# The first level of a score tree taken from TensorE to GpSimd and VectorE, and the order around four points of TensorE's first rounds changed

## The chip, the cores and the metric

The kernel runs on one core of a Trainium2 chip. The metric is the device time of one execution in microseconds (us), the median of several. A "span" is the time from the first to the last instruction in one profiled execution, some 2 us less than the device time. All executions used below ran fast, unless one is called slow.

## The reference, cut to what matters

Attention of the RWKV6 kind over 4 batches, 8 heads, 768 steps and head size 48, then a normalisation and an MLP (384 to 1536 to 384), all in fp32.

```python
for t in range(S):
    cur = u * (k_t outer v_t)
    y[:, :, t] = r_t @ (state + cur)
    state = w_t[:, None] * state + k_t outer v_t
x = y as (B, S, H*D)
out = x + relu(layernorm(x) * g @ w_ch1) @ w_ch2
```

What matters: for an odd step t, the step just before it contributes (r_t . k_{t-1}) v_{t-1}. No decay w stands between two neighbours. All earlier steps come in with products of w.

## The kernel before: the parts concerned

There are eight rounds of 384 steps (a batch and a half of its steps). A round has two units of four heads. In a round the scores of steps inside blocks of 64 are built as a tree of six levels. Level 0 holds the neighbours, level 1 pairs of pairs, and so on. At each level TensorE multiplies (`quads`, into `a_ps`), VectorE multiplies r and k by the next products of w (`grow`, into `rkT`) and puts the scores into a matrix A (`keep`). The MLP of the round before (`h_ps`, `o_ps`) is cut into steps that fill TensorE between the levels.

```python
def own_products(q, eng):              # r*k*u of step t itself
    rk = st[q]["ruk"] = p1.tile([P, TT, NH, D], F32, tag="rk", ...)
    eng.tensor_tensor(out=rk, in0=k_of(q), in1=r_of(q), op=mult)     # names shortened
    eng.tensor_tensor(out=rk, in0=rk, in1=u_bc[...], op=mult)

def own_sums(q):
    o = st[q]["own"] = p4.tile([P, TT, NH], F32, tag="own", ...)
    DVE.tensor_reduce(out=o, in_=st[q]["ruk"], axis=AX.X, op=ALU.add)

def own_term(q, eng):                  # vo = v * own, added to y later
    eng.tensor_tensor(out=a["vo"], in0=vn[q], in1=own broadcast, op=mult)
...
for lev in range(NLEV):                # one round
    ...                                # states, outputs and MLP steps of the round before
    for q in now:
        if slot:
            quads(q, lev)
    ... grow(q, lev) ; keep(rnd, lev)
    ...
    if rnd == 2 and lev == 2:
        for q in now:
            take(DVE, q)               # own_products and own_sums, both on VectorE
    ...
    if lev == NLEV - 1 and rnd >= 2:   # what is prepared for the next round
        tasks += each(own_term, new[:1], [POOL])
        tasks += each(own_products, new[1:], [POOL])
        tasks += each(own_sums, new[1:]) + each(own_term, new[1:], [POOL])
        tasks += each(totals, [rnd + 1], [POOL])
```

The program fixes the order of instructions on each engine, so on VectorE a sum that waits for GpSimd's products holds up all that stands behind it. Two buffers named `nat["w"]`, which hold w as it lies in memory, have no use once round 1 has begun.

## Time and profile before

| | before |
|---|---|
| device time, median of the 3 runs known when predicting | 581.06 us (580.58 to 582.94) |
| span of the profiled execution | 579.2 us |
| busy: TensorE, VectorE, GpSimd | 560.5, 317.3, 94.5 us |
| mean granted clock of TensorE | 0.979 |

The busy time of TensorE is 97% of the span, so two things can shorten it: work taken from TensorE, and the stops and half-clock stretches of the first 217 us. The views that show both, line by line, are in the prediction. In the costliest groups, the columns after the bar are busy us and mean ns of one instruction:

```profile
L49 DVE TENSOR_TENSOR rkT<-rkT,wT 128x768 f32<-128x768 f32 x16 | 17.1, 1107 | 0.9 <-PE a_ps L49 0.8
```

This is `grow` of level 0. Two such products stand between a round's start and its level 1, and they read the tiles while GpSimd works beside them.

### The profile page before, as it was taken

The numbers are of one execution on the slowest core, as the hardware profiler recorded it, in microseconds if no ns is written. First come the engines' busy times: TensorE is split into PE (matmuls) and PEld (weight loads), VectorE is DVE, ScalarE is ACT, GpSimd is POOL, SyncE is SP. The second block draws the span as 40 slices with busy tenths as digits, with TensorE's granted clock in tenths as the row PEclk, the third lists the DMA queues.
The fourth block names the chain that finished last, engine by engine and source line by source line (L and its number), as shares of the span: only waits on it lengthen the run. The fifth ranks groups of instructions, "written<-read, shape, count | busy, mean of one in ns | idle before, by whom it ended". The sixth has DMA issues, their size and how long they took to land.

```text
span 579.2 us, 19006 instructions
## 1 busy us (share of the span) xinstructions
PE 560.5 (97%) x8378; PEld 370.7 (64%) x8378; DVE 317.3 (55%) x636; ACT 168.6 (29%) x363; POOL 94.5 (16%) x127
## 2 busy tenths in 40 slices
PE   9999989999979989999999999999999999999997
PEld 6776765666546656666666666666666666666554
DVE  4879888769767754558256654557253531130000
ACT  3576597402340015201241015301331025202200
POOL 6140010204062007100350007020420000000000
PEclk9889799999997989999999999999999999999999
DMA  9848587245564547345343534144000000000000
GB/s 231 194 114 166 124 234 179 53 93 101 147 135 89 132 98 138 68 115 120 95 86 82 134 85 89 36 116 103 15 3 2 15 29 2 1 15 29 0 14 27
DMA packets 109875, 50.78 MB, mean 88 GB/s; under 512 B 92768, under 2 KB 99040, under 8 KB 109792
## 3 DMA queue, kind: packets, MB, share of 16 engines
q1 hardware_dynamic: 107920, 48.98, 37.1%
q8 instruction: 65, 1.06, 0.8%
q10 hardware_dynamic: 1872, 0.59, 0.4%
q14 instruction: 18, 0.15, 0.1%
HBM read 42.76 MB, written 4.72 MB: 82 GB/s over the span
## 4 chain that ended last, share of the span: by engine, by line
PE 81%; DVE 6%; ACT 4%; SPq 3%; DMA 3%; issue 2%; POOL 0%; ACTq 0%; DVEq 0%
PE o_ps L49 30%; PE h_ps L49 27%; PE a_ps L49 10%; PE y L49 4%; DVE rkT L49 3%; PE kv L49 2%; SPq L163 2%; DMA v<-in_v_dram 2%; PE kn_ps L49 2%; PE xT_ps L49 1%; ACT rest L49 1%; PE own_ps L49 1%; SPq L173 1%; PE idle L49 1%; PE r_ps L49 1%
## 5 line engine op out<-in xcount | busy, mean ns | idle before, releaser
L49 PE MATMUL o_ps<-w_sb,h 128*128 128x384 f32 x576 | 201.0, 498 | 1.0 <-ACT h L49 1.0
L49 PE MATMUL h_ps<-xT,w_sb 128*128 128x384 f32 x576 | 197.3, 494 | 0.0
L49 PEld LDWEIGHTS o_ps<-w_sb,h 128*128 128x128 f32 x576 | 107.3, 193 | 67.9 <-issue 3.0
L49 PEld LDWEIGHTS h_ps<-xT,w_sb 128*128 128x128 f32 x576 | 106.7, 191 | 66.7 <-issue 1.2
L49 DVE TENSOR_TENSOR rkT<-rkT,tot 128x768 f32<-128x768 f32 (+1 forms) x96 | 79.3, 867 | 28.3 <-issue 15.5
L49 ACT ACTIVATE h<-h_ps 128x384 f32<-128x384 f32 x96 | 46.8, 488 | 151.3 <-PE h_ps L49 151.2
L49 PEld LDWEIGHTS a_ps<-rkT 48*64 48x64 f32 x4608 | 73.7, 137 | 24.3 <-issue 15.9
L49 PE MATMUL a_ps<-rkT 48*64 48x32 f32 x4608 | 79.1, 222 | 3.7 <-DVE s L49 3.0
L49 DVE TENSOR_TENSOR o<-o_ps,x 128x384 f32<-128x384 f32 x24 | 13.3, 555 | 103.2 <-PE o_ps L49 103.1
L49 POOL TENSOR_TENSOR vo<-v,own 128x576 f32<-128x576 f32 x16 | 19.2, 1203 | 258.5 <-DVE own L49 217.7
L49 DVE SCALAR_TENSOR_TENSOR s<-s,decay,kv 128x48 f32<-128x48 f32 x160 | 29.3, 258 | 33.9 <-PE kv L49 33.9
L49 ACT ACTIVATE rstd<-mv,eps 128x3 f32<-128x3 f32 x8 | 2.4, 296 | 134.8 <-DVE mv L49 134.8
L49 DVE COPY_PREDICATED A<-mask,a_ps 128x768 f32<-128x768 int8 x32 | 38.3, 1195 | 0.0
L49 DVE TENSOR_TENSOR x<-y,vo 128x288 f32<-128x288 f32 x32 | 13.2, 453 | 37.4 <-PE y L49 37.3
L49 ACT ACTIVATE xT<-xT_ps,g_sb 128x384 f32<-128x384 f32 x24 | 13.7, 580 | 55.3 <-PE xT_ps L49 55.3
L49 DVE TENSOR_REDUCE own<-rk 128x12 f32<-128x576 f32 x12 | 8.9, 746 | 20.6 <-POOL rk L49 20.6
L49 DVE TENSOR_SCALAR w_sb<-w_sb 128x384 f32<-128x384 f32 (+1 forms) x48 | 18.6, 388 | 0.8
L49 DVE STREAM_TRANSPOSE rkT<-r_runs 128x384 f32<-128x384 f32 x20 | 15.7, 837 | 4.3 <-DMA r_runs<-in_r_dram 4.3
L49 PEld LDWEIGHTS kv<-v,kn 64*64 64x64 f32 x768 | 12.7, 134 | 8.2 <-issue 6.2
L49 PEld LDWEIGHTS y<-v,A 64*64 64x64 f32 x384 | 13.3, 137 | 7.1 <-issue 4.4
L49 DVE TENSOR_TENSOR rkT<-rkT,wT 128x768 f32<-128x768 f32 x16 | 17.1, 1107 | 0.9 <-PE a_ps L49 0.8
L49 DVE STREAM_TRANSPOSE rkT<-k_runs 128x384 f32<-128x384 f32 x20 | 15.8, 849 | 1.7 <-DMA k_runs<-in_k_dram 1.6
(82 smaller groups left out, 501.4 us busy)
## 6 DMA issues: line engine op xcount, KB each, us to landing
raw<-in_moe_w_ch_dram SPq DMA_DIRECT2D x24, 384.0 KB, 3.7
w_runs<-in_w_dram SPq DMA_DIRECT2D x79, 70.0 KB, 2.1
k_runs<-in_k_dram SPq DMA_DIRECT2D x79, 70.0 KB, 2.0
r_runs<-in_r_dram SPq DMA_DIRECT2D x79, 70.0 KB, 2.0
v<-in_v_dram SPq DMA_DIRECT2D x48, 96.0 KB, 3.0
out_dram<-o SPq DMA_DIRECT2D x24, 192.0 KB, 2.8
nat_r<-in_r_dram SPq DMA_DIRECT2D x42, 96.0 KB, 3.3
nat_k<-in_k_dram SPq DMA_DIRECT2D x42, 96.0 KB, 3.2
```

The source lines that it names most:

```text
L49: return lambda *args, **kw: self.tc.keep_in_program_order(f(*args, **kw))
L163: eng.dma_start(out=t[ds(HP * j + SQ * e, SQ), 0:n], in_=bass.AP(tensor=src.tensor, offset=first + SQ * e, ap=[[NS * D, SQ], [1, n]]),)
L173: eng.dma_start(out=vn[q][:, c], in_=steps(v, q, c))
```

## The change

Two things are done at once. From round 3 on (FIRST = 3), level 0 leaves TensorE: k and v are loaded again one step back into the two idle buffers, GpSimd multiplies k_{t-1} by r_t, VectorE sums over the head size and zeroes the even steps, and GpSimd multiplies v_{t-1} by the sum and adds it to the term of the step itself. Apart from that, the order is changed at four points: the own sums of round 1 (A), an MLP step in round 2 (B), GpSimd's products at the end of round 2 (C), and the normalisation in rounds 3 to 7 (D).

```diff
+    def load_before(q, src, i, eng=SP):        # k or v, one step back
+        ...  out=nat["w"][i][:, c, :, 0:D],  offset = ... + (... - 1) * D
     def own_products(q, eng):
+        if q >= FIRST * U:
+            k1 = nat["w"][0][..., 0:D]
+            eng.tensor_tensor(out=k1, in0=k1, in1=nat["r"][q % 2][..., 0:D], op=ALU.mult)
     def own_sums(q):
+        if q >= FIRST * U:
+            o = st[q]["next"] = p2.tile([P, TT, NH], F32, tag="next", ...)
+            DVE.tensor_reduce(out=o, in_=nat["w"][0][..., 0:D], axis=AX.X, op=ALU.add)
+            DVE.tensor_scalar(out=o, in0=o, scalar1=odd, scalar2=None, op0=ALU.mult)
     def own_term(q, eng):
+        if q >= FIRST * U:                     # v1 = v1 * next;  vo = vo + v1
+            eng.tensor_tensor(out=v1, in0=v1, in1=a["next"] broadcast, op=ALU.mult)
+            eng.tensor_tensor(out=a["vo"], in0=a["vo"], in1=v1, op=ALU.add)
     def keep(rnd, lev):
+        if lev == 0 and rnd >= FIRST:          # memset of A's odd columns in rounds 3 and 4
+            ...
+            return
     ...
             for q in now:
-                if slot:
+                if slot and (lev or rnd < FIRST):
                     quads(q, lev)
 # B, round 2
-                if lev < 2:
-                    mlp_step()
+                    if lev or q == old[-1]:    # inside the loop over the two units
+                        mlp_step()
 # A, round 1: taken out here ...
-                if lev == 1:
-                    tasks += each(product_sums, now)
 # ... and mixed among the transposes and MLP steps
+                    each(product_sums, now) if lev == 1 else [],
 # D
-                    tasks += each(norm, [rnd - 1])
+                    tasks = each(norm, [rnd - 1]) + tasks
 # C, and the loads
+                if new:
+                    load_before(new[0], k, 0)
+                    load_before(new[0], v, 1)
+            if lev == 4 and rnd > 1:
                 tasks += each(own_products, new[:1], [POOL])
-                if rnd > 2 and new:
+                if rnd >= 2 and new:
                     own_sums(new[0])
-                if rnd == 2:
-                    tasks += each(own_products, new[:1], [POOL]) + each(own_sums, new[:1])
                 if rnd >= 2:
+                    tasks += each(load_before, new[1:], [k], [0])
                     tasks += each(own_term, new[:1], [POOL])
+                    tasks += each(load_before, new[1:], [v], [1])
```

More of the change, by code (lines that the diff above doesn't have):

```diff
@@ L168, in stage @@
                 )
+    def load_before(q, src, i, eng=SP):
+        b, f, g = units[q]
+        for c in range(TT):
+            eng.dma_start(
+                out=nat["w"][i][:, c, :, 0:D],
+                in_=bass.AP(
+                    tensor=src.tensor,
+                    offset=src.offset + ((b * H + g * NH) * S + f * RN + c * P - 1) * D,
+                    ap=[[D, P], [S * D, NH], [1, D]],
+                ),
+            )
     def load_v(q, eng=SP):
@@ L409, in own_sums @@
         DVE.tensor_reduce(out=o, in_=st[q]["ruk"], axis=AX.X, op=ALU.add)
+        if q >= FIRST * U:
+            o = st[q]["next"] = p2.tile([P, TT, NH], F32, tag="next", name=f"next{q}")
+            DVE.tensor_reduce(out=o, in_=nat["w"][0][..., 0:D], axis=AX.X, op=ALU.add)
+            DVE.tensor_scalar(out=o, in0=o, scalar1=odd, scalar2=None, op0=ALU.mult)
     def products(q, eng=DVE):
@@ L445, in own_term @@
         )
+        if q >= FIRST * U:
+            v1 = nat["w"][1][..., 0:D]
+            eng.tensor_tensor(
+                out=v1, in0=v1,
+                in1=a["next"][:, :, :, None].broadcast_to([P, TT, NH, D]), op=ALU.mult,
+            )
+            eng.tensor_tensor(out=a["vo"], in0=a["vo"], in1=v1, op=ALU.add)
     a_ps = {}
@@ L487, in keep @@
         n = 1 << lev
-        A, ps = a_bufs[rnd % 2], a_ps[rnd]
+        A = a_bufs[rnd % 2]
+        if lev == 0 and rnd >= FIRST:
+            if rnd < FIRST + 2:
+                DVE.memset(
+                    A.rearrange("s j u k (q two) -> s (j u k) q two", two=2)[..., 1], 0.0
+                )
+            return
+        ps = a_ps[rnd]
         if lev == NLEV - 1:
@@ L759, in units_of @@
         return [U * rnd + g for g in range(U)] if rnd < NR else []
+    FIRST = 3
+    odd = const.tile([P, 1], F32, name="odd")
     def take(eng, q):
@@ L904 @@
                 tasks += each(load_v, now)
+                DVE.tensor_reduce(
+                    out=odd, in_=ident.rearrange("p (q two) -> p q two", two=2)[:, :, 1],
+                    axis=AX.X, op=ALU.add,
+                )
             if rnd == 2 and lev == 2:
@@ L964 @@
                 n = (1, 2, 2, 1, 0, 0)[lev] * NP
-                tasks += mixed([begin] * BEGINS[lev], [join] * JOINS[lev], ahead[:n])
+                tasks += mixed(
+                    [begin] * BEGINS[lev], [join] * JOINS[lev], ahead[:n],
+                    each(product_sums, now) if lev == 1 else [],
+                )
                 del ahead[:n]
```

## The prediction

> **What bounds the kernel now.** I read the page first: the busy shares, then the rows of 40 slices.
>
> ```profile
> PE 560.5 (97%) x8378; PEld 370.7 (64%) x8378; DVE 317.3 (55%) x636; ACT 168.6 (29%) x363; POOL 94.5 (16%) x127
> ...
> PE   9999989999979989999999999999999999999997
> ...
> PEclk9889799999997989999999999999999999999999
> ```
>
> TensorE (PE) is the bound: 18.7 us idle of a span of 579.2. VectorE (DVE) has 45% of its time free, GpSimd (POOL) 84%. The clock row shows the second loss: dips to 7 or 8 in slices 2, 3, 5, 13 and 15 (14.5 us each), none after 217 us. So time is to be had in two ways: TensorE work taken out anywhere, and stops and half-clock stretches in the first 217 us.
>
> Next, the chain of waits in order of time (start, us, what). From 217 us on it is nearly all TensorE, and one round of the attention (384 steps of 8 heads) reads like this; the last round to be drained, at 484 us, has no score matmuls between:
>
> ```profile
> 226.69 0.84 PE kv L49 x48
> 227.53 1.39 PE a_ps L49 x96
> 228.92 7.94 PE h_ps L49 x24
> ...
> 484.10 0.84 PE kv L49 x48
> 484.94 7.94 PE h_ps L49 x24
> ```
>
> The a_ps block is level 0 of the score tree, the thing removed. Beside it the same neighbours follow each other without it, and take as long (0.84 and 7.94). So one block costs exactly its 1.39 us. Cutting the trace into rounds shows how full they are (start:end and length, then busy us of PE, PEld, DVE, ACT, POOL, then clock, DMA share, GB/s):
>
> ```profile
> 226.60:291.00 64.40, 64.34 (x1034) 42.21 (x1034) 35.87 (x70) 14.73 (x33) 13.04 (x13) 1.00 0.48 104
> 291.00:355.30 64.30, 64.24 (x1018) 42.14 (x1017) 37.58 (x74) 14.71 (x33) 12.76 (x13) 1.00 0.43 97
> ```
>
> Then the timeline around the early dips (start, us, engine, what, and in brackets the idle time before and its releaser):
>
> ```profile
> 59.08 3.68 PE L49 MATMUL own_ps<-sel,ruk 128*128 128x2 f32 x24
> 62.62 4.19 PE L49 MATMUL h_ps<-xT,w_sb 128*128 128x384 f32 x6
> ```
> ```profile
> 118.39 0.26 PE L49 MATMUL y<-s,rkT 48*64 48x48 f32 x2 [1.01 <-issue]
> ```
> ```profile
> 167.03 0.75 DVE L49 TENSOR_REDUCE own<-rk 128x12 f32<-128x576 f32 x1 [4.11 <-POOL rk L49]
> 169.69 3.06 DVE L49 TENSOR_TENSOR rkT<-rkT,wT 128x768 f32<-128x768 f32 x2
> 169.88 0.91 PE L49 MATMUL kv<-v,kn 64*64 64x48 f32 x48 [0.90 <-PE h_ps L49]
> 173.78 2.79 PE L49 MATMUL a_ps<-rkT 48*64 48x32 f32 x96 [2.98 <-DVE s L49]
> ```
> ```profile
> 206.64 1.73 PE L49 MATMUL xT_ps<-ident,xn 128*128 128x128 f32 x6 [2.10 <-DVE xn L49]
> 208.16 3.54 PE L49 MATMUL o_ps<-w_sb,h 128*128 128x384 f32 x6
> ```
>
> Four places. A (59 us, round 1): 24 matmul records with only two moving columns, then six h_ps matmuls in 4.05 us (the chain's figure) where full clock takes 1.94. B (117 us, round 2): a stop of 1.01. C (170 us, start of round 3): stops of 0.90 and 2.98, then a_ps in 2.79 instead of 1.53 at a clock of 0.50, and the next six o_ps in some 4.1 instead of 2.13. D (204 us, round 3): a stop of 2.10, then six o_ps in 3.33 to 3.5 instead of 1.94.
>
> **What the Trainium skill says.** "TensorE: Matmul & The Clock Gate", Part 1: the clock has two states, half and full, chosen by the activity in a window of about 3.4 us. The trace agrees in part: half clock follows A, C and D and was 0.50 in 173.8 to 176.6, but D's stop was only 2.10 us, shorter than that window, while B's 1.01 and one of 0.89 at 154 us cost no clock. "GPSIMD Engine Reference", section 4.1: elementwise work with two inputs is about twice as slow on GpSimd as on VectorE. The trace agrees: the multiply k by r took 1.42 us on GpSimd at its quickest, 0.75 on VectorE. "SBUF — State Buffer", "Who interferes with whom": a VectorE instruction with two SBUF inputs and a GpSimd one that reads SBUF block each other. The trace agrees: the pair rkT<-rkT,wT took 1.82 at 229 us and 3.06 at 169.69 beside GpSimd's totals.
>
> **The change part by part.**
>
> 1. Level 0 by GpSimd and VectorE, rounds 3 to 7. The program order shows ten groups of 24 matmuls gone, two in each of five rounds. In rounds 4 to 7 that is 4 x 1.39 = 5.6 us of TensorE's time, on the path, as those rounds are 99.9% TensorE. Round 3's is counted under C.
>
> What is added: twelve loads a round of 96 KB (nat_k took 3.2 us to land; issuing three took 1.5, so SyncE gets 6 us more of a 64 us round, at a DMA share of 0.3 to 0.5). GpSimd: three more operations a unit. At 1.41 for the product and 1.15 to 1.4 for each of the other two, this is 4.1 a unit, 8.2 a round, 41 us in all: POOL goes from 94 to about 136 us, about 23%. VectorE: a reduction of 0.75 and a tiny multiply of about 0.1 a unit, 1.7 a round, less A<-a_ps,bits at 0.95 (a memset stands there in rounds 3 and 4 only): net +0.7 in a round of 36 of 64.
>
> What could put this on the path is order: VectorE works in order, and waits for GpSimd's product of the second unit. Before, it waited 4.12 us there in a round (reduction at 218.9, the next at 223.77). Now the first unit's sums end at about 220.5, GpSimd then does three operations (about 3.9) and three more (4.2), so the second unit's sums end near 229 instead of 224.5. Then s (1.84) and the two products by w (1.8 to 3.1) end near 233 to 234. TensorE needs them for level 1, after kv and 24 h_ps: 226.7 + 0.84 + 7.94 + 0.84 = 236.3. So 2 to 3 us of slack are left: hidden.
>
> 2. A: the two sets of own-sums matmuls are set apart by h_ps and transposes. They stay 24, about 3.0 us at full clock (12 took 1.43 to 1.50 elsewhere) against 3.61; h_ps saves 4.05 - 1.94 = 2.1, the w transposes 1.36 - 0.82 = 0.5. Sum 3.2. But VectorE converts weights all through here: from 57 to 92 us it was idle for one wait of 2.61 only. It can't get ahead by more than that, so I count 2.0.
>
> 3. B: a step of six o_ps records (2.1 us) now stands between the two y groups: 1.0 gained.
>
> 4. C: the first unit's GpSimd products move to level 4 and its sums ahead of the last transposes, so that VectorE waits less. I work it out again. Sums of the first unit end at 157.3 (after rkT, done at 155.74). The last r_runs still lands at 161.5. GpSimd ends own_term at 160.5 and the second unit's two products at 163.3; its third waits for the shifted k, issued after r_runs at 160.1 to 161.6, landing near 164.4; done 165.8. VectorE's second sums end at 166.7 (before: 167.78), s at 168.9, the first product by w near 170.6, as GpSimd is in its way. TensorE, 2.0 us ahead without level 0 and free of the 0.90 wait, reaches level 1 at 167.9. So the stop does not go: it shrinks from 3.88 in two pieces to about 2.7, and still costs clock. Level 1 starts at 170.6 instead of 173.78: 3.2 gained, round 3's level 0 included.
>
> 5. D: norm is put ahead of the transposes. The averages end at 202.66; with 0.3 for the root and 1.26 for xn it is done at 204.4, as TensorE gets there (204.54). Gained: 2.1 + 1.5 = 3.6. In rounds 4 to 7 the same order takes away a wait of 0.25 (at 271.5) each: 1.0.
>
> Sum: 5.6 + 2.0 + 1.0 + 3.2 + 3.6 + 1.0 = 16.4. 581.06 - 16.4 = 564.7. New small waits in a changed order usually give some back; I take off about one us and say 565.5.
>
> **The rivals.** First: VectorE's wait for GpSimd takes the place of what was removed. For it: it already waits 4.1 us a round, C is made of that, and port blocking can stretch GpSimd's now twelve operations. Against: the slack of 2 to 3 us above, and before, no wait of TensorE over 0.3 in rounds 4 to 7. If 2 us a round came back, with some lost clock, the gain would be about 7: 574. Second: the shifted loads stand in SyncE's one queue, waiting for VectorE and GpSimd, and hold up w_runs behind them. For it: fifteen w_runs issues of some 0.47 come after the shifted v. I estimate them at 290 to 297 us of the old clock, needed near 305 for the transposes. Against: 5 us of slack. If late, 1 to 3 us a round: 568 to 576. Third: C is cured entirely, with its clock (3.2 more): 562. Fourth: A gives nothing, for VectorE and ScalarE were the limit: 567.5.
>
> **Range and chances.** The removed blocks (7.0 with round 3's) are nearly certain, D likely (85%), A, B and the 0.25s some 70 to 80%. Faster by over 2% needs 569.4 or less, so 4.7 us of 16.4 may be lost. Time 565.5 us, 8 in 10 between 559.5 and 571. Chances: faster 0.77, same 0.22, slower 0.01.
>
> **What would show it.** Right: rounds 4 to 7 cut in the trace at 62.6 to 62.9 us each instead of 64.3, TensorE still 99% busy; no stop before xT_ps near 200 us and full clock after it; h_ps after own_ps at 1.94; no wait between the y groups; a stop of 2 to 4 us left at the start of round 3, with a half-clock stretch; POOL at 130 to 140 us busy. Wrong: TensorE waiting for s or rkT at each round's start, with VectorE waiting on GpSimd's nat_w or on DMA before it; w_runs transposes waiting on DMA; or rounds at 64 us.

## The result, and the profile after

| | before | after |
|---|---|---|
| device time, median of 4 runs | 582.0 us (580.58 to 583.5) | 566.33 us (565.84 to 566.87) |
| ratio, with 95% interval | | 0.9731 (0.9700 to 0.9761) |
| span, clock | 579.2 us, 0.979 | 564.6 us, 0.988 |

The ratio here and below is the mean time of one kernel's fast runs over that of the other's in the same rounds, so it is not quite the ratio of the medians. The kernel became 2.7% faster, and the predicted 565.5 us is within a microsecond. First the page of the changed kernel, in the rows that were shown of the one before:

```profile
PE 548.6 (97%) x7898; PEld 359.3 (64%) x7898; DVE 332.1 (59%) x654; ACT 168.7 (30%) x363; POOL 134.8 (24%) x157
...
PE   9999998998889999999999999999999999999997
...
PEclk9899999999997999999999999999999999999999
```

TensorE lost 480 records of matmuls (96 in each of five rounds) and 11.9 us. GpSimd rose from 94.5 to 134.8 us. Of the five dips in the clock row two remain, and one, in slice 13, is as deep as before. Slices 10 and 11 (127 to 155 us) have got lower digits in the PE row than before, which no step of the prediction had in it.

Next the chain of waits after 217 us, and two rounds cut as in the prediction (start:end and length, then busy us of PE, PEld, DVE, ACT, POOL, clock, DMA share, GB/s):

```profile
218.56 0.84 PE kv L49 x48
219.41 7.94 PE h_ps L49 x24
```
```profile
218.50:281.00 62.50, 62.50 (x934) 40.68 (x933) 40.00 (x75) 14.60 (x32) 21.62 (x19) 1.00 0.55 122
281.00:343.60 62.60, 62.60 (x918) 40.69 (x917) 39.66 (x78) 14.77 (x33) 22.24 (x19) 1.00 0.56 122
```

The a_ps block between kv and h_ps is gone, its neighbours take what they took, and TensorE has no idle time in these rounds at a full clock. GpSimd went from 13 to 22 us a round and did not stop TensorE in them. How near it came shows at the start of round 4, in VectorE's pair of `grow` (timeline) and TensorE's level 1 (chain):

```profile
222.56 4.00 DVE L49 TENSOR_TENSOR rkT<-rkT,wT 128x768 f32<-128x768 f32 x2
```
```profile
228.19 0.84 PE a_ps L49 x57
```

The pair ends at 226.56, which is 1.6 us before level 1 begins.

Now the first rounds. Place A, in the timeline of TensorE (start, us, engine, what, idle time before in brackets):

```profile
62.86 1.40 PE L49 MATMUL own_ps<-sel,ruk 128*128 128x2 f32 x12
...
64.48 2.10 PE L49 MATMUL h_ps<-xT,w_sb 128*128 128x384 f32 x6
...
66.75 1.40 PE L49 MATMUL own_ps<-sel,ruk 128*128 128x2 f32 x12
```

Twelve matmuls with two columns, then six h_ps in 2.10 us in place of 4.19: the clock stayed full. Place B in the timeline is further on than it was; the wait between the two outputs is gone, but 19 us later there is a new one. TensorE and then VectorE of the changed kernel:

```profile
132.98 2.20 PE L49 MATMUL h_ps<-xT,w_sb 128*128 128x384 f32 x6
136.55 4.14 PE L49 MATMUL h_ps<-xT,w_sb 128*128 128x384 f32 x12 [1.37 <-DVE o L49]
```
```profile
132.87 0.76 DVE L49 TENSOR_TENSOR rk<-nat_k,nat_r 128x576 f32<-128x576 f32 x1
133.66 1.59 DVE L49 TENSOR_TENSOR rk<-rk,u_bc 128x576 f32<-128x576 f32 x1
135.28 0.75 DVE L49 TENSOR_REDUCE own<-rk 128x12 f32<-128x576 f32 x1
135.95 0.55 DVE L49 TENSOR_TENSOR o<-o_ps,x 128x384 f32<-128x384 f32 x1
```

The same work of TensorE in the kernel before, with no wait in it:

```profile
136.20 6.12 PE L49 MATMUL h_ps<-xT,w_sb 128*128 128x384 f32 x18
```

On VectorE, `o` stands behind both `take` calls of round 2 (products and sums; the first three of these four VectorE lines are the second call). TensorE comes to these h_ps one MLP step further on than before, and now it is there before `o` is done.

Place C, the start of round 3, first TensorE, then VectorE, then one line of GpSimd:

```profile
166.07 0.92 PE L49 MATMUL kv<-v,kn 64*64 64x48 f32 x48
168.66 0.90 PE L49 MATMUL a_ps<-rkT 48*64 48x32 f32 x48 [1.68 <-DVE rkT L49]
170.71 1.50 PE L49 MATMUL a_ps<-rkT 48*64 48x32 f32 x48 [1.15 <-DVE rkT L49]
172.15 8.61 PE L49 MATMUL o_ps<-w_sb,h 128*128 128x384 f32 x18
```
```profile
162.02 0.75 DVE L49 TENSOR_REDUCE own<-rk 128x12 f32<-128x576 f32 x1 [1.13 <-POOL rk L49]
163.88 0.75 DVE L49 TENSOR_REDUCE next<-nat_w 128x12 f32<-128x576 f32 x1 [1.11 <-POOL nat_w L49]
...
166.89 3.77 DVE L49 TENSOR_TENSOR rkT<-rkT,wT 128x768 f32<-128x768 f32 x2
```
```profile
162.43 1.42 POOL L49 TENSOR_TENSOR nat_w<-nat_w,nat_r 128x576 f32<-128x576 f32 x1 [0.45 <-DMA nat_w<-in_k_dram]
```

The stops of 0.90 and 2.98 have become 1.68 and 1.15, and the half clock is still there: 18 o_ps in 8.61 us, where 6.07 is a full clock's. VectorE waits twice for GpSimd, the second time for a product whose shifted k landed late, and then the pair of `grow` takes 3.77 us. Place D:

```profile
200.77 0.88 PE L49 MATMUL xT_ps<-ident,xn 128*128 128x128 f32 x6
201.48 2.10 PE L49 MATMUL o_ps<-w_sb,h 128*128 128x384 f32 x6
```

No wait ahead of the transposes, and a full clock after them (0.88 and 2.10; before, 1.73 and 3.54).

To compare kernels by stage I cut each trace at the same events of TensorE: the first level 1 of round 1 (called a1), the first o_ps, the first kv of round 3, of round 4 and of the drained round. How long the start before a1 takes differs from one execution to the next of the same program (55.9 and 57.7 us in two profiles of the changed kernel, 55.6 to 60.8 over all kernels, which have the same instructions up to there). From a1 on, the two profiles of the changed kernel (after and after_again) agree to 0.11 us (506.90 and 506.79). So the column "a1 to end" is the finer measure here, and the timed medians the coarser one. It is not exact, though. The two profiles share out the same time differently between the stages around round 3's start, by 0.7 us. And where the own-sums matmuls stand together as before (A undone), the first stage took 35.31, 35.48 and, in level0_only, 33.54 us with the same instructions: there the half clock behind them lasted one step of 3.41 us, in the others two. I read stage differences of under some 0.7 us as noise, and those of kernels with A undone as uncertain by nearly 2 us.

| kernel | device time, median | a1 to first o_ps | to round 3 | round 3 | rounds 4 to 7 | a1 to end |
|---|---|---|---|---|---|---|
| before | 582.0 | 35.31 | 67.40 | 66.36 | 257.41 | 521.65 |
| after | 566.33 | 32.91 | 68.33 | 59.56 | 250.84 | 506.90 |
| order_only | 566.80 | 33.03 | 68.60 | 55.20 | 256.40 | 508.43 |
| level0_only | 576.38 | 33.54 | 70.16 | 66.95 | 251.84 | 517.70 |
| undo_a | 568.15 | 35.48 | 68.21 | 59.86 | 250.85 | 509.68 |
| undo_d | 571.03 | 32.91 | 68.56 | 63.76 | 251.84 | 512.30 |
| late_sums | 563.69 | 33.03 | 68.28 | 57.63 | 250.85 | 504.99 |
| first_4 | 561.82 | 33.11 | 68.23 | 54.66 | 250.85 | 502.05 |
| late_take | 562.10 | 32.81 | 65.27 | 57.26 | 250.85 | 501.44 |
| first_4_take | 561.34 | 32.97 | 65.25 | 58.67 | 250.84 | 502.99 |
| late_first_4_take | 559.86 | 32.81 | 65.26 | 58.03 | 250.85 | 502.20 |
| pool_1 | 567.88 | 32.78 | 68.16 | 60.46 | 250.85 | 507.52 |
| after_again | 564.50 | 32.85 | 69.04 | 58.83 | 250.85 | 506.79 |

From before to after, the stages give 2.40, -0.93, 6.80 and 6.57, and with -0.09 in the drained round that is the 14.75 us of the last column.

### The profile page after: what moved, and what is told of

Read it like the earlier page. It is cut to its first block, busy times and chain, and to the rows that moved or that the text cites. A ratio compares the mean times of both kernels' runs of the same rounds, so it can differ in the third digit from the quotient of the medians.

```text
span 564.6 us, 18202 instructions
## 1 busy us (share of the span) xinstructions
PE 548.6 (97%) x7898; PEld 359.3 (64%) x7898; DVE 332.1 (59%) x654; ACT 168.7 (30%) x363; POOL 134.8 (24%) x157
## 4 chain that ended last, share of the span: by engine, by line
PE 82%; DVE 9%; ACT 3%; DMA 2%; issue 2%; SPq 1%; POOL 0%; ACTq 0%; DVEq 0%; POOLq 0%
PE o_ps L49 33%; PE h_ps L49 27%; PE a_ps L49 9%; PE y L49 5%; DVE rkT L49 3%; DVE w_sb L49 2%; PE kv L49 2%; PE kn_ps L49 2%; DMA nat_r<-in_r_dram 1%; ACT rest L49 1%; PE xT_ps L49 1%; PE own_ps L49 1%; PE idle L49 1%; PE k_ps L49 1%; DVE A L49 1%
## 5 line engine op out<-in xcount | busy, mean ns | idle before, releaser
L49 DVE TENSOR_TENSOR rkT<-rkT,tot 128x768 f32<-128x768 f32 (+1 forms) x96 | 77.4, 849 | 27.6 <-issue 17.6
L49 PEld LDWEIGHTS a_ps<-rkT 48*64 48x64 f32 x4128 | 65.7, 137 | 23.5 <-issue 12.5
L49 PE MATMUL a_ps<-rkT 48*64 48x32 f32 x4128 | 70.7, 221 | 3.4 <-DVE rkT L49 3.3
L49 POOL TENSOR_TENSOR nat_w<-nat_w,nat_r 128x576 f32<-128x576 f32 x10 | 14.4, 1436 | 103.1 <-DMA nat_w<-in_v_dram 70.5
L49 DVE TENSOR_TENSOR rkT<-rkT,wT 128x768 f32<-128x768 f32 x16 | 24.9, 1591 | 0.9 <-PE a_ps L49 0.8
L49 POOL TENSOR_TENSOR tot<-wT 128x768 f32<-128x768 f32 x6 | 12.4, 2072 | 20.2 <-DVE rkT L49 20.2
```

The source lines that it names most:

```text
L49: return lambda *args, **kw: self.tc.keep_in_program_order(f(*args, **kw))
```

## The experiments

All are variants of the changed kernel, and all gave correct results. Four at a time ran on one chip beside the kernel before, which took 580.98, 578.67 and 579.91 us (medians) in the three sets. My first theory was the prediction's: 7.0 of the 16.4 us come from TensorE's work removed, the rest from the four places. The rivals were that the order alone does nearly all, or that level 0 gives back what it takes.

**order_only: the new order, level 0 left on TensorE.**

```diff
-    FIRST = 3
+    FIRST = 99
     # and the load_before calls taken out
```

> The changed order alone: level 0 stays with TensorE in all rounds, no shifted loads, no added GpSimd or VectorE work. Theory (the parts add up): five level-0 blocks of 1.39 us come back, 7 us, so about 573.3 us, and rounds 4 to 7 at 64.1 us each (64.3 less the 0.25 us wait before xT_ps). Rival (the new order only pays because TensorE has less to do): near 580 us.

Measured: 566.80 us (565.85 to 569.68), ratio 0.977 (0.9733 to 0.9808). The theory (573.3) missed by 6.5 us and the rival (580) by more: the order alone does nearly all. The time is within what timing can tell of the whole change; by the table, level 0's move adds 508.43 - 506.90 = 1.5 us. In rounds 4 to 7 it saves what it should: 256.40 - 250.84 = 5.56, which is 4 x 1.39. But round 3 is 4.36 us shorter without it. The start of round 3 in this kernel, TensorE and VectorE:

```profile
167.79 1.56 PE L49 MATMUL a_ps<-rkT 48*64 48x32 f32 x96
169.29 6.07 PE L49 MATMUL o_ps<-w_sb,h 128*128 128x384 f32 x18
```
```profile
160.37 0.70 DVE L49 TENSOR_REDUCE own<-rk 128x12 f32<-128x576 f32 x1
...
162.97 3.07 DVE L49 TENSOR_TENSOR rkT<-rkT,wT 128x768 f32<-128x768 f32 x2
```

No stop before level 1, full clock after it, no wait of VectorE for GpSimd. So the order alone would have cured place C (only 0.72 us of waiting stands a little earlier, at level 0), and what keeps the stop there is level 0's own work on GpSimd and VectorE.

**level0_only: the reverse, level 0 moved and the four places in the old order.**

```diff
     # A, B, C and D as in the kernel before; load_before, k1, next, v1 and FIRST = 3 kept
```

> The kernel before with level 0 of rounds 3 to 7 given to GpSimd and VectorE and nothing else moved. Theory (the parts add up): rounds 4 to 7 lose 1.39 us each (62.9 us a round), the start of round 3 changes by 0 to 2 us, as VectorE's wait for GpSimd sets it; 575 to 577 us. Rival (VectorE's wait for GpSimd takes the place of the removed matmuls): over 579 us, with TensorE waiting for rkT at the round starts.

Measured: 576.38 us (574.81 to 580.48), ratio 0.9936 (0.9891 to 0.998). Rounds 4 to 7 give 5.57 us. Round 3 gives nothing (66.95 against 66.36), with a stop of

```profile
173.47 1.50 PE L49 MATMUL a_ps<-rkT 48*64 48x32 f32 x48 [5.04 <-DVE rkT L49]
```

and the stage ahead of it is 2.76 us longer. The trace shows in what: TensorE waits 1.93 before `kn_ps` instead of 0.89, behind VectorE's transposes, which wait for loads of k and r, and the next six h_ps run at half clock.

```profile
152.88 0.88 PE L49 MATMUL kn_ps<-ident,rkT 128*128 128x128 f32 x6 [1.93 <-DVE rkT L49]
...
154.74 3.46 PE L49 MATMUL h_ps<-xT,w_sb 128*128 128x384 f32 x6
```

TensorE came to this place early, as its first stage was 1.77 shorter than the kernel before's with the same instructions, but what it waited for came only 0.7 earlier (counted from a1, these `kn_ps` start at 96.18; before, at 96.86). So most of the 2.76 fits a lead that the loads took back and the half clock that followed; it is not shown to be a cost of level 0. Level 0 alone is worth 521.65 - 517.70 = 3.95 us, the order alone 13.22, and both together 14.75, not 17.17. The total of 2.4 that they lose together says little, since the first stage of level0_only is in it. In round 3 alone, where the order's cure and the new work meet, they lose 3.8: the order gains 11.16 there, level 0 loses 0.59, and both together gain 6.80.

**undo_a and undo_d: one place put back.**

```diff
 # undo_a
+                if lev == 1:
+                    tasks += each(product_sums, now)
-                    each(product_sums, now) if lev == 1 else [],
 # undo_d
-                    tasks = each(norm, [rnd - 1]) + tasks
+                    tasks += each(norm, [rnd - 1])
```

> The changed kernel with the two groups of own-sums matmuls of round 1 together again. Theory (round 2's VectorE and load chain swallows what round 1 gains: 3.2 us ahead after part B, 1.3 us ahead at the end of round 2): under 1 us lost, 566 to 567.3 us, although TensorE gets its half clock after own_ps back and reaches the o_ps of round 1 about 2 us later. Rival (A is worth its full 2.2 us): 568.5 us.

> The changed kernel with the normalisation behind the transposes again. Theory (stop of 2.1 us, xT_ps 0.9 longer, o_ps 1.4 longer at half clock, and 0.25 us in each of rounds 4 to 7): 4.4 + 1.0 more, about 571.7 us, with a stop before xT_ps of round 3 and a clock near 0.6 after it. Rival (the half clock there came from the round's start and not from this stop): 2.1 + 1.0 more, 569.4 us.

Measured, undo_a: 568.15 us (566.58 to 569.67), ratio 0.9784 (0.9747 to 0.9821). The first stage is 2.57 us longer, the whole from a1 on 2.78. The matmuls of two columns are back together, and so is the half clock behind them:

```profile
57.85 3.36 PE L49 MATMUL own_ps<-sel,ruk 128*128 128x2 f32 x18
61.06 4.19 PE L49 MATMUL h_ps<-xT,w_sb 128*128 128x384 f32 x6
```

The theory (round 2 swallows it, under 1 us lost) is false, and its rival is right: A is real. VectorE's conversion of weights, for which the prediction had cut A from 3.2 to 2.0, swallows little. The size of A depends on the half clock: level0_only, with A undone as well, has a first stage only 0.6 longer than the changed kernel's. Putting A back leaves the stage to round 3 as it was (68.21) and longer than before the change (67.40), so what the changed kernel loses there is hardly A's lead taken back. Measured, undo_d: 571.03 us (569.47 to 572.07), ratio 0.9831 (0.9795 to 0.9866). Round 3 is 4.20 longer and rounds 4 to 7 together 1.00, which is 0.25 each. Both places do what the prediction says, and somewhat more.

**late_sums: the second unit's sums and term are put behind level 0 of the next round, so that VectorE doesn't wait for GpSimd ahead of `grow`.**

```diff
+                if lev == 0 and rnd >= FIRST:
+                    own_sums(now[1])
+                    own_term(now[1], POOL)
-                    tasks += each(own_sums, new[1:]) + each(own_term, new[1:], [POOL])
```

> The changed kernel, with the second unit's sums (VectorE) and own term (GpSimd) moved behind the next round's first growth, so that VectorE does s and the products by w without waiting for GpSimd. Theory (the stop at the start of round 3 is VectorE standing in order behind GpSimd's products of the second unit): no stop before level 1 of round 3, no half clock after it, round 3 from kv to kv at 53 to 54 us instead of 59.6; about 560 us in all. Rival (GpSimd blocks VectorE's products at the shared port, whatever stands before them): the two products by w still take 3.7 us or more, a stop over 1.5 us stays, round 3 at 57 us or more, 564 us or more.

Measured: 563.69 us (559.31 to 564.52), ratio 0.9717 (0.9677 to 0.9757), a1 to end 504.99. Round 3 is 1.93 shorter than after, not the 6 or so that the theory promised for a cured C. C was cured. In stretches of round 3's start, first the changed kernel and then this one (columns as above):

```profile
166.00:182.00 16.00, 13.17 (x247) 8.87 (x248) 13.54 (x28) 2.11 (x5) 9.35 (x10) 0.79 0.69 149
```
```profile
166.00:182.00 16.00, 16.00 (x326) 10.81 (x319) 15.86 (x30) 0.86 (x2) 9.49 (x10) 1.00 0.65 137
```

TensorE is busy all through and the clock is 1.00 in place of 0.79. The pair of `grow` still took 3.89 us, so a `grow` made slow by GpSimd is not enough to stop TensorE: what stops it is VectorE's wait for GpSimd's products of the second unit standing in front. But D was back:

```profile
195.78 1.83 PE L49 MATMUL xT_ps<-ident,xn 128*128 128x128 f32 x6 [2.15 <-DVE xn L49]
197.40 3.43 PE L49 MATMUL o_ps<-w_sb,h 128*128 128x384 f32 x6
```

TensorE comes to D earlier than in the changed kernel, and VectorE had waited 1.13 and 2.25 us for two loads of r ahead of xn (in order_only, 0.61 for one). The theory was right about C, and the expectation missed what the earlier arrival of TensorE would meet.

**first_4: level 0 moved from round 4 on only.**

```diff
-    FIRST = 3
+    FIRST = 4          # and the loads only where the next round needs them,
+                       # round 4's first ones issued in program order
```

> The changed kernel, with level 0 of round 3 given back to TensorE (GpSimd takes it from round 4 on; no shifted loads before). Theory (moving level 0 costs more than it saves only in round 3, where r_runs are late and VectorE has no slack; from round 4 on it is hidden): round 3 at 55.2 us as with the order alone, rounds 4 to 7 at 62.7 each, about 562 us. Rival (the first round on GpSimd always pays): round 4 gets 4 us longer instead, about 566 us.

Measured: 561.82 us (560.84 to 563.71), ratio 0.9706 (0.9672 to 0.974). Theory right: round 3 takes 54.66 us, near order_only's 55.20, and rounds 4 to 7 take 250.85, as after. This shows the split most cleanly: with level 0 moved in one round less, the kernel is 4.85 us faster from a1 on, although TensorE does 96 records of matmuls more.

**late_take: late_sums, and the second `take` of round 2 put one level later, behind `o`.**

```diff
             if rnd == 2 and lev == 2:
-                for q in now:
-                    take(DVE, q)
-                    tasks += each(load, new[q % U :][:1], "kr")
+                take(DVE, now[0])
+                tasks += each(load, new[:1], "kr")
+            if rnd == 2 and lev == 3:          # as the last tasks
+                tasks += each(take, [DVE], now[1:]) + each(load, new[1:], "kr")
```

> The kernel with the late sums, and VectorE's own products of round 2's second unit moved one level later, behind the o that h_ps waited 1.37 us for in round 2. Theory (that stop is only VectorE's order): 1.4 us less than with the late sums alone, about 558.6 us, no wait of h_ps for o. Rival (round 2 is set by the chain of w_runs, k_runs and r_runs loads through VectorE's transposes): the 1.4 us come back as a longer wait of kn_ps for rkT, no gain, 560 us or more.

Measured: 562.10 us (559.41 to 564.14), ratio 0.9714 (0.9677 to 0.9751). The stage to round 3 takes 65.27 us against 68.28 in late_sums, so the place of `take` was worth 3.0. That is more than the wait of 1.37: a second one, 1.18 before the last transposes of the round (`kn_ps`, released by VectorE's rkT), is gone too. The h_ps that waited:

```profile
131.44 6.07 PE L49 MATMUL h_ps<-xT,w_sb 128*128 128x384 f32 x18
```

So the stop was VectorE's order, but the 558.6 us were missed, for round 3 has stops again (0.89 and 1.15, then 18 o_ps in 7.64). The trace shows what VectorE waited for ahead of `s` and `grow`:

```profile
156.16 0.86 DVE L49 STREAM_TRANSPOSE rkT<-r_runs 128x384 f32<-128x384 f32 x1 [2.19 <-DMA r_runs<-in_r_dram]
158.29 0.86 DVE L49 STREAM_TRANSPOSE rkT<-r_runs 128x384 f32<-128x384 f32 x1 [1.26 <-DMA r_runs<-in_r_dram]
```

The last of these starts 102.03 us after a1, against 102.99 in late_sums. So the loads of r did not come later: TensorE came some 3 us earlier, and they only 1.0.

**pool_3 and pool_1: GpSimd's load by itself.** In the changed kernel the product k by r of the second unit is repeated three times, or once, with the same result.

```diff
-        eng.tensor_tensor(out=rk, in0=k_of(q), in1=r_of(q), op=ALU.mult)
+        for _ in range(1 + (3 if q >= FIRST * U and q % U else 0)):      # 1 in pool_1
+            eng.tensor_tensor(out=rk, in0=k_of(q), in1=r_of(q), op=ALU.mult)
```

> The changed kernel, with GpSimd's product k by r of the second unit done four times instead of once in rounds 3 to 7 (same result), 4.2 us more GpSimd work ahead of VectorE's second sums. Theory (VectorE stands behind GpSimd with about 1.6 us to spare at the starts of rounds 4 to 7, none in round 3): stops of about 2.6 us and some half clock in each of rounds 4 to 7, and 4 us more in round 3: 578 to 586 us. Rival (GpSimd is hidden, three quarters of its time are free): under 568 us.

> The changed kernel with one extra product k by r of the second unit on GpSimd, 1.4 us ahead of VectorE's second sums, in rounds 3 to 7. Theory (1.6 us to spare at the starts of rounds 4 to 7): rounds 4 to 7 together stay at 250.8 us, round 3's stop grows by about 1 us, 567 to 568 us. Rival (each us of GpSimd shows): 5 times 1.4, 573 us or more.

Measured, pool_3: 582.45 us (580.87 to 590.68, one of the six slow), ratio of its fast runs 1.0051 (1.0014 to 1.0089). The time lies in the theory's range. Three products of 1.41 us, 4.2 us a round in five rounds, cost all that the change had gained. Its profile fell in a slow execution, so I don't split it. Measured, pool_1: 567.88 us (566.8 to 568.33), ratio 0.9785 (0.9734 to 0.9836). The theory held here too: rounds 4 to 7 take 250.85 us as without it, and round 3 is 0.90 longer than in the first profile of the changed kernel. So the slack of a round's start lies between 1.4 and 4.2 us, and the 1.6 us read off above fit. The prediction had 2 to 3.

**first_4_take, and late_first_4_take: can the gains be added up?** The first is first_4 with the `take` of late_take; the second has the late sums of rounds from 3 on as well.

```diff
 # first_4_take:       first_4 + the two hunks of late_take's take
 # late_first_4_take:  first_4_take + late_sums (for rnd >= 3)
```

> Level 0 on GpSimd from round 4 on, and VectorE's own products of round 2's second unit one level later. Theory (the two gains are in different stretches and add up): round 2's part at 65.3 us instead of 68.2, round 3 at 54.7, rounds 4 to 7 at 250.8, about 559 us. Rival (with TensorE 3 us further ahead VectorE becomes the bound at round 3's start, as in the run with late sums and late products): a stop before level 1 of round 3 and half clock, round 3 at 57 us, 561 us or more.

> The same with the second unit's sums behind the next round's first growth, from round 3 on. Theory (VectorE then has nothing of GpSimd's to wait for before rkT): no stop before level 1 of round 3, 558 to 559 us. Rival (VectorE only does the sums later and is late for xn in round 3): a stop before xT_ps of round 3 as with the late sums, 561 us or more.

Measured: 561.34 us (560.51 to 565.48), ratio 0.9686 (0.9641 to 0.9732), and 559.86 us (558.83 to 561.99), ratio 0.9656 (0.9609 to 0.9703). Neither adds up: both theories failed, and of the first run's rival the stop and the half clock came. The 3 us at `take` are gained in both (65.25 and 65.26), but round 3 gives them back: 58.67 and 58.03 against 54.66 in first_4. In the second, the waits stand at level 0 of round 3, and half clock follows:

```profile
157.67 0.55 PE L49 MATMUL a_ps<-rkT 48*64 48x32 f32 x24 [1.21 <-DVE s L49]
158.15 7.77 PE L49 MATMUL h_ps<-xT,w_sb 128*128 128x384 f32 x18
```

late_first_4_take has the lowest median of all, and beats the kernel before and the changed one (its slowest run, 561.99, lies below the changed kernel's fastest of the same set, 563.0). From a1 on, first_4, late_take and it lie within 0.8 us of each other, so which of these three is best is not settled.

**after_again: the changed kernel once more, in the third set.**

> The changed kernel once more, unchanged, on the chip and beside the runs of these kernels. Theory (only the start of the kernel varies from run to run, with where the free clock windows fall): 565 to 568 us, the time from level 1 of round 1 to the end again 506.9 us within 0.5 us. Rival (stops and half clock later on vary too): that time differs by over 1 us.

Measured: 564.50 us (563.0 to 565.65), ratio 0.9732 (0.969 to 0.9774), against 0.9731 the first time. The time from a1 on is as expected (506.79), the median 0.5 us below the range. The medians differ by 1.8 us between the two sets, the ratios do not.

## Why the prediction was right, point by point

The time, the direction and the range are right. By the steps:

Rounds 4 to 7, predicted 5.6 for the blocks and 1.0 for the waits of 0.25: measured 6.57. order_only and undo_d separate the two as 5.56 and 1.00. "Hidden" holds there for GpSimd's and VectorE's new work, with 1.6 us of slack instead of 2 to 3: the pair of `grow` took 4.00 us, for which the prediction had 1.8 to 3.1. GpSimd's 136 us were 134.8.

A, predicted 2.0, is 2.4 in the change and 2.6 to 2.8 when undone (0.6 by level0_only's first stage, where the half clock was short). The fourth rival, that A gives nothing, is false. D, predicted 3.6, is 4.4 (round 3's 6.80 less C's 2.4): undone it costs 4.2, and the sum had left out the transposes themselves, which ran at half clock too (1.73 against 0.88).

C, predicted 3.2, gave 2.4 (from the round's kv to its outputs 24.12 before, 21.74 after). The mechanism was right: VectorE behind GpSimd's third product, which waits for the shifted k, leaves a stop, said to be about 2.7 and measured as 1.68 + 1.15. That level 1 was to start at 170.6 and its second half started at 170.71 is partly luck: VectorE's second sums were done at 165.0 and not 166.7, TensorE was there at 167.0 and not 167.9, level 1's first half started at 168.66, and the second half waited for a pair of `grow` that took 3.77 us. The term mis-sized is the clock behind it: the 18 o_ps took 8.54 us in the chain where they had taken 7.89, which gives back 0.65.

B is the step that failed. "1.0 gained" was read from the wait between the outputs alone. It went, but TensorE stood at another wait of 1.37 further on, and the wait before `kn_ps` grew from 0.89 to 1.20, so the stage became 0.93 longer (1.64 in after_again). The 1.37 (1.36 to 1.38) stands in every kernel with B and the old `take`, order_only among them (68.60), so it isn't the shifted loads, and undo_a among them, so it isn't A's lead. It is missing before, in level0_only, which has no B, and where `take` is moved. B alone was not undone, so its share of the 0.93 is read from waits and not measured. The rule that a step taken earlier is missing later had been stated for the sum ("new small waits"), not for this place.

So the sum of 16.4, less one, met 14.75 (15.7 by the medians) partly because errors cancel: B and C came 2.7 short, A and D 1.2 over.

A second thing the prediction got wrong is not in the total. It credits level 0's move with 7.0 of the 16.4 us, as "nearly certain". The runs show 1.5 us net on top of the order, for in round 3 the work moved keeps VectorE, and with it TensorE, waiting: a version that leaves round 3 alone is 4.85 us faster. The first rival, "VectorE's wait for GpSimd takes the place", was set against rounds 4 to 7 and is false there; it is true in round 3, where one of the two waits is for a shifted k that has only just landed. The second rival, SyncE's queue, shows in no later round. The third, C cured, is what the order alone does.

What stays open: what the shifted loads cost by themselves, since no run has them without the products (a late load of r or k stands ahead of most of the stops left at round 3's start), and how much of level0_only's 2.8 before round 3 is level 0's own.

## What to carry to other kernels

Work taken from a full engine is worth its time only where the engines that take it have slack before that engine needs their next result: read this slack at each stage's first dependent instruction, not from busy shares (GpSimd was at 24% and had 1.6 us). A change made everywhere may be right in four rounds and wrong in one, so try its first round as a parameter. When an order removes a wait, look for the instruction that this engine now reaches earlier, and compare stages between the same events of two traces, since the start of an execution can vary by more than the effect.

## What the Trainium skill lacked or had wrong

- "TensorE: Matmul & The Clock Gate", Part 1, gives a window of about 3.4 us for the loss of clock, idle or busy. It also calls the window free-running, and the traces agree: in each, the half-clock stretches start and end on one grid with steps of 3.41 us. What it does not give is how much idle time in a window is enough. Here half clock followed single stops of 2.10 and 2.15 us (D), two stops of 1.68 and 1.15 with 0.9 of work between (C), and two of 0.44 and 1.21; a single one of 1.37 cost none. My reading of these, not tested alone: what counts is how little work falls into one step of the grid, not one idle gap of the window's length.
- The same page and part say nothing of work that is dense but tiny. 24 matmul records with two moving columns, without idle time, in 3.68 us, brought six h_ps at half speed (4.19 us); 12 and 12 with other matmuls between left them at 2.10. Twelve are not always safe: near 19 us, where 12 stand right beside score matmuls, half clock followed in 10 of the 14 traces.
- "SBUF — State Buffer", "Who interferes with whom", names the pair that block each other; the sizes it gives (6.8 and 1.5 times slower) are not said to be for such a pair. Here the pair of VectorE products `rkT<-rkT,wT` took 1.82 us at its quickest, 3.06 to 4.28 beside GpSimd's work; the mean of one rose from 1107 to 1591 ns with the change, and GpSimd's first product of the totals from 1466 to 2072 ns.
- "GPSIMD Engine Reference", section 4.1, gives one factor of about two for two inputs. Measured on GpSimd at 128 x 576: 1.41 us with two full inputs (0.75 on VectorE), 1.15 with one input broadcast along the last axis.
- "TensorE: Matmul & The Clock Gate", Part 1, says that a free-running window makes the first transition vary by 500 ns either way between runs. Here the time to the same instruction was 55.6 to 60.8 us, more than most of the effects tested. It goes with the number of half-clock steps of 3.41 us before it: 55.6 to 56.0 us with none, 55.8 to 57.1 with one, 57.6 to 58.0 with two, 59.1 with three, 60.8 with four.
